# ConvNeXt-V2 block on one core: three expansions between two bursts of the convolution, statistics early, Gram in halves, a new pace for the second stage

## The chip, the cores and the metric

One core of one Trainium2 chip. The metric is device time in microseconds (us), the median over the executions of a kernel. The executions of the kernel before agree within about 0.6% in each set of measurements. Engines are named as in the profile: PE is TensorE, PEld its weight loads, ACT ScalarE, DVE VectorE, POOL GpSimd, SP SyncE.

## The reference, cut to what matters

```python
# x: 512 x 512 pixels, C = 96 channels, bf16; E = 4 * C = 384
out = depthwise_conv_3x3(x, dw)
h = layernorm_over_channels(out)          # no scale, no shift
h = gelu_tanh(h @ w1)                     # 96 -> 384
gx = sqrt(sum_over_all_pixels(h * h) + 1e-6)      # one number per channel of h
nx = gx / (mean(gx) + 1e-6)
h = grn_gamma * (h * nx) + grn_beta + h
return x + h @ w2                         # 384 -> 96
```

`gx` needs every pixel, so the kernel has two stages. Stage 1 computes `h` for the whole image for its squares, and keeps a quarter of it (half of the last two blocks). Stage 2 computes the rest of `h` anew ("recompute"), and then multiplies by `w2`.

## The kernel before

Stage 1 is a loop over slots. A slot handles four image rows (a "block") in each part of the pipeline:

- the convolution of one block on TensorE, in three bursts of 24 small matmuls into the one PSUM buffer `Y`; ScalarE then copies it to `y_bf`;
- the statistics of the layer norm (`stage_stats`), 24 small matmuls that add into the sums `S`;
- for an earlier block the expansion by `w1`: six groups of 1024 columns, called p0, p1, p2 (`pair`, GELU to `gsh`) and r0, r1, r2 (`rest`, GELU to `gm`). They go through the pool `U`, which has two buffers, so a group's matmuls wait for the GELU of the group two before;
- the squares: `bn_stats` on VectorE for most of `h`, and the diagonal of a Gram product on TensorE (`gram_mms`) for the rest. A block has 12 or 24 Gram matmuls; every third slot has 24.

`S` and `gram` are slices of one tile, `SG`.

```python
SG = psS.tile([128, 2 * NS + NCH * 128], f32, name="SG")
S = SG[:, :2 * NS].rearrange("p (h s) -> p h s", h=2)
gram = SG[:, 2 * NS:].rearrange("p (j e) -> p j e", j=NCH)
...
def burst(n):                            # convolution, 24 matmuls
    ...
    if n < 2:
        pe.drain()                       # bursts n and n+1 add to the same sums
...
def stage_moments(k):                    # once in a batch of four blocks
    dve.tensor_scalar(out=m[:, :, :N], in0=S[:, :, :N], scalar1=1.0 / C, ...)
    dve.memset(S[:], 0.0)                # the sums start anew
...
def combine(b):                          # every twelfth slot: aggregate bn_stats
    for k in sorted(bsts):
        if b == NBLK - 1 or ents[b + 1] >= 32 * (k + 1):
            for j in range(NCH):
                dve.bn_aggr(...)
```

The slot itself, in program order; each engine keeps this order in stage 1:

```python
for k in get("moments"):
    stage_moments(k)                     # at the start of the slot after the batch's last statistics
...
conv(0); pair(0); pair(1); squares(0)
conv(1); turn_x(s + 2)                   # transposes of the input on VectorE
pair(2); squares(1)
conv(2); evac()                          # y_bf
rest(0); squares(2); stage_stats(b2)
rest(1); gram_mms(b2)
rest(2); squares_rest()
combine(b)
```

Stage 2, for each block `n`: start the loads of block n + 5, add the bias to the residual on GpSimd (`xb`), then 4 groups of 12 output matmuls (`O`), each evacuated by VectorE (`o_sb`) with `xb` added. After each group, `pace` issues as many recompute units (three matmuls and one GELU of 1536 columns) as are due; a block has three.

```python
def pace(n, sub):
    due = sum(1 for v in todo if v <= n + 1) if sub == NSUB - 1 else 0
    even = LEAD + (n * NSUB + sub + 1) * (total + 2 - LEAD) / (NSUB * NBLK)
    advance(max(due, even), n + PRE)
...
for n, q in enumerate(ORDER):
    if n + PRE < NBLK:
        stage_load(n + PRE, nc.sync, nc.gpsimd)     # on GpSimd: gl (one block in three), then xr
    if n + 2 < NBLK:
        stage_xb(ORDER[n + 2], nc.gpsimd, B2c)
    o_sb = stage_mm2(n, q)                          # calls pace
```

In stage 1 all engines go through a wrapper that keeps the program's order (`InOrder`, here `pe`, `dve`, `act`, `pool`). The calls above use `nc.gpsimd` itself, so there the framework may order GpSimd's instructions as it sees fit.

Of the kernel before, what the change touches and what calls it, by code (L numbers as in the profile page):

```python
# [53 lines left out]
def kernel(  # L54
# [17 lines left out]
    E = w1.shape[1]  # L72
# [5 lines left out]
    NBLK = H // GR  # L78
# [81 lines left out]
    with ExitStack() as p1:  # L160
# [74 lines left out]
        NSUB = PXP // GPS  # L235
# [80 lines left out]
        LEAD = RES * UPB + 2  # L316
        todo = [n for n in range(NBLK) for _ in range(UPB)]
        total = len(todo)
# [10 lines left out]

        def pace(n, sub):  # L330
            due = sum(1 for v in todo if v <= n + 1) if sub == NSUB - 1 else 0
            even = LEAD + (n * NSUB + sub + 1) * (total + 2 - LEAD) / (NSUB * NBLK)
            advance(max(due, even), n + PRE)

        SG = psS.tile([128, 2 * NS + NCH * 128], f32, name="SG")
# [1 line left out]
        gram = SG[:, 2 * NS:].rearrange("p (j e) -> p j e", j=NCH)  # L337
# [15 lines left out]
        n = 0  # L353
# [54 lines left out]
        def conv_taps(b, spare):  # L408
            if spare:
                Ua = psU.tile([128, 2, W], f32, name="U")  # L410
                Ub = psU.tile([128, 2, W], f32, name="U")
                Y = [Ua[:, 0, :], Ua[:, 1, :], Ub[:, 0, :]]
            else:
                Y3 = psY.tile([128, NI, W], f32, name="Y")
                Y = [Y3[:, i, :] for i in range(NI)]
            mms = []
            for n in range(3):
                mms.append([(h, j, (n + h) % NI, dx) for dx in (0, -1, 1) for j in range(GR) for h in range(2)])
            flat = [m for ms in mms for m in ms]
            first = {}  # L420
            last = {}
            for n, (h, j, i, dx) in enumerate(flat):
                first.setdefault((i, j), n)
                last[i, j] = n

            def burst(n):
                k = sum(len(ms) for ms in mms[:n])
                for h, j, i, dx in mms[n]:
                    src = b + shift(h, j)
                    o0, o1 = max(0, -dx), W - max(0, dx)  # L430
                    pe.matmul(
                        Y[i][32 * j:32 * j + 32, o0:o1],
                        lhsT=Wq[64 * h:64 * h + 64, i, dx + 1, j, :],
                        rhs=x_rows(src, 64 * h, 64 * h + 64, i, MB * (1 + dx) + o0, o1 - o0)
                        if 0 <= src < NBLK else zrow[64 * h:64 * h + 64, o0:o1],
                        start=first[i, j] == k,
                        stop=last[i, j] == k,
                    )
                    k += 1
                if n < 2:  # L440
                    pe.drain()

            def evac():
                y = ypool.tile([128, NI, W], bf16, name="y_bf")
                if spare:
                    act.activation(out=y[:, 0:2, :], in_=Ua[:], func=ACTF.Identity)
                    act.activation(out=y[:, 2, :], in_=Ub[:, 0, :], func=ACTF.Identity)
                else:
                    act.activation(out=y[:], in_=Y3[:], func=ACTF.Identity)
                ybf[b] = y  # L450

            return [lambda n=n: burst(n) for n in range(3)], evac

        def stage_sq(b, on_act):
            q = ysqpool.tile([128, NI, W], bf16, name="ysq")
# [152 lines left out]
        def px0(b):  # L608
            return NCH * QW * (cm_quads(b) - 2)
# [51 lines left out]

            return pair, rest, squares, squares_rest, store

        def gram_mms(b):
            for k in range((TAIL - px0(b)) // E):
                for j in range(NCH):
                    c = px0(b) + k * E + j * 128
                    v = gms[b][:, c:c + 128]
                    pe.matmul(gram[:, j, :], lhsT=v, rhs=v, start=False, stop=True, skip_group_check=True)
# [51 lines left out]
        for s in range(last_slot + 1):  # L721
            get = lambda kind: at.get((s, kind), [])
            if s + 4 < NBLK:
                load_x(s + 4)
            for b in get("read"):
                stage_read(b)
            for b in get("write"):
                stage_write(b)
            for k in get("bcast"):
                stage_bcast(k)  # L730
            for k in get("rows"):
                stage_rows(k)
            if store:
                store()
                store = None
            for k in get("moments"):
                stage_moments(k)
            for k in get("newton"):
                stage_newton(k, pool)
            for b in get("norm"):  # L740
                stage_norm(b)
            for b in get("sqp"):
                stage_sq(b, False)
            for k in get("rstd"):
                stage_rstd(k, pool)
            mlp = get("mlp")

            def spread_out():
                for k in get("spread"):
                    stage_spread(k)  # L750
                for b in get("norma"):
                    stage_norm(b)

            spare = not mlp and s % 2 == 1
            taps, evac = conv_taps(s, spare) if s < NBLK else ([], None)
            if not mlp:
                for f in taps:
                    f()
                if not spare:
                    spread_out()  # L760
                if evac:
                    evac()
                for b in get("sqa"):
                    stage_sq(b, True)
                if s + 2 < NBLK:
                    turn_x(s + 2)
                for b in get("stats"):
                    stage_stats(b)
                if spare:
                    spread_out()  # L770
                for k in get("chain"):
                    stage_moments(k)
                    stage_chain(k)
                for k in get("turn"):
                    stage_turn(k)
                for b in get("gram"):
                    gram_mms(b)
            else:
                b = mlp[0]
                pair, rest, squares, squares_rest, put_out = mlp_units(b)  # L780
                conv = lambda n: taps[n]() if taps else None
                conv(0)
                pair(0)
                pair(1)
                if not taps:
                    for b2 in get("gram"):
                        if b2 != b:
                            gram_mms(b2)
                squares(0)
                conv(1)  # L790
                spread_out()
                if s + 2 < NBLK:
                    turn_x(s + 2)
                pair(2)
                squares(1)
                for k in get("turn"):
                    stage_turn(k)
                conv(2)
                if evac:
                    evac()  # L800
                rest(0)
                squares(2)
                for b2 in get("stats"):
                    stage_stats(b2)
                rest(1)
                if taps:
                    for b2 in get("gram"):
                        if b2 != b:
                            gram_mms(b2)
                rest(2)  # L810
                squares_rest()
                for b2 in get("gram"):
                    if b2 == b:
                        gram_mms(b2)
                if not is_res(b):
                    store = put_out
            if s == 1:
                setup_mlp()
            if s == 4:
                setup_rest()  # L820
            for b in get("combine"):
                combine(b)
            if s == last_slot - 3:
                pc.close()
                late.psO = p2.enter_context(tc.tile_pool(name="psO", side="right", bufs=2, space=bass.MemoryType.PSUM))
                late.xr = p2.enter_context(tc.tile_pool(name="xr", side="right", bufs=5))
                late.xb = p2.enter_context(tc.tile_pool(name="xb", side="right", bufs=3))
                late.gr = p2.enter_context(tc.tile_pool(name="gr", side="right", bufs=4))
                late.gl = p2.enter_context(tc.tile_pool(name="gld", side="right", bufs=6))
                late.o = p2.enter_context(tc.tile_pool(name="o", side="right", bufs=4))  # L830
            for n in {2: (0, 1, 2), 1: (3, 4)}.get(last_slot - s, ()):
                stage_load(n, sp, pool)
            if s == last_slot - 1:
                for n in range(RES):
                    stage_xb(ORDER[n], pool, B2bc_f)
# [104 lines left out]
```

## Time and profile before

| | before |
|---|---|
| time, median of the first measurement | 1564.21 us |
| stage 1, to the first `o_sb` | 1031.6 us |
| stage 2, from there to the end | 531.6 us |
| slots of stage 1, in turn | 7.45, 7.46, 7.63 us |
| period of `xb` on GpSimd in stage 2 | 4.09 us |

The stages and periods are read from start times in the trace. The page of the kernel before begins so (busy us, share of the span, instructions):

```profile
span 1563.2 us, 55720 instructions
...
PE 1450.2 (93%) x23749; PEld 844.8 (54%) x23749; DVE 1129.5 (72%) x2027; ACT 1447.1 (93%) x1306; POOL 1314.2 (84%) x933
```

TensorE and ScalarE are both at 93%, which does not tell what bounds a slot. ScalarE's timeline does (start, duration, engine, source line, operation, count, and in brackets the idle time before it and what ended that):

```profile
502.31 2.93 ACT L32 ACTIVATE gsh<-U 128x1024 bf16<-128x1024 f32 x3 [0.55 <-PE U L32]
505.13 1.45 ACT L32 ACTIVATE y_bf<-Y 128x1536 bf16<-128x1536 f32 x1
506.47 2.85 ACT L32 ACTIVATE gm<-U 128x1024 bf16<-128x1024 f32 x3
509.75 2.92 ACT L32 ACTIVATE gsh<-U 128x1024 bf16<-128x1024 f32 x3 [0.42 <-ACT gm L32]
```

Every slot has one hole of 0.42 to 0.56 us, before p0. The loop behind it: r2 waits for a buffer until r0's GELU is done, then TensorE does r2, burst 0 with its drain, and p0, while ScalarE has only r1 and r2 to do.

The next lines are TensorE, VectorE and ScalarE in a slot that follows aggregations.

```profile
532.31 2.92 ACT L32 ACTIVATE gsh<-U 128x1024 bf16<-128x1024 f32 x3 [0.44 <-ACT gm L32]
...
532.58 2.76 DVE L32 BATCH_NORM_AGGREGATE mv<-bst 128x2 f32<-128x192 f32 x3
...
535.26 0.23 DVE L32 TENSOR_SCALAR mom<-SG 128x128 f32<-128x128 f32 x1
...
535.59 0.17 DVE L32 MEMSET SG<- 128x128 f32 x1
...
535.81 0.44 PE L32 MATMUL SG<-rowsel,y_bf 128*128 128x4 bf16 x12 [0.28 <-DVE SG L32]
```

VectorE does the three aggregations first (2.76 us), then reads and clears the sums (`mom`, MEMSET). The clear ends 3.45 us after p0's GELU began. The statistics, which add to these sums, come just then and wait 0.28 us. Over 600 us that wait is all but nothing (us in total, times, longest):

```profile
PE SG L32 <- DVE SG L32: 2.0, 7, 0.3
```

At the end of stage 2 ScalarE starves. The pace before hands out 378 units over 512 groups, a little under three per block, so the lead of recompute over the output matmuls melts away:

```profile
1537.35 4.13 ACT L32 ACTIVATE gr<-U 128x1536 bf16<-128x1536 f32 x3 [1.40 <-PE U L32]
```

### The profile page before, as it was taken

How to read it: one execution, taken by the hardware profiler on the slowest of the kernel's cores; microseconds unless marked ns; L12 is line 12 of the kernel's file. 1: busy time of each engine (PE TensorE's matmuls, PEld its weight loads, DVE VectorE, ACT ScalarE, POOL GpSimd, SP SyncE). 2: the span in 40 equal slices, each digit the busy share in tenths (PEclk: the TensorE clock that was granted, in tenths of full speed). 3: DMA queues.
4: the chain of work that ended last, by engine and by line, in shares of the span. 5: the costliest groups of instructions: out<-in, count | busy, mean ns of one | idle time of the engine just before them, and what ended most of it. 6: DMA issues, size and time to landing. Idle time of an engine off the chain costs nothing. (4 is left out here: it accounts for less than half of the span.)

```text
span 1563.2 us, 55720 instructions
## 1 busy us (share of the span) xinstructions
PE 1450.2 (93%) x23749; PEld 844.8 (54%) x23749; DVE 1129.5 (72%) x2027; ACT 1447.1 (93%) x1306; POOL 1314.2 (84%) x933
## 2 busy tenths in 40 slices
PE   7888999999999999999999997789999999999997
PEld 3444444444444444444444444457777777777765
DVE  6748978888898888889888888855555555555544
ACT  3889989999999999999999999989999999999997
POOL 3559888998989898998889897459999999999994
PEclk9999999999999999999999999999999999999999
DMA  5668787787778677777778667869999999999993
GB/s 148 182 182 269 224 262 217 240 254 227 225 234 259 210 249 244 230 235 237 247 210 243 213 197 230 268 238 387 393 379 396 387 397 388 383 381 388 379 372 147
DMA packets 235470, 427.94 MB, mean 274 GB/s; under 512 B 34102, under 2 KB 148374, under 8 KB 235222
## 3 DMA queue, kind: packets, MB, share of 16 engines
q1 hardware_dynamic: 219972, 356.59, 70.2%
q0 software_dynamic: 13888, 67.64, 11.4%
q8 instruction: 186, 3.05, 0.8%
q14 instruction: 62, 0.51, 0.1%
q10 hardware_dynamic: 1362, 0.15, 0.1%
HBM read 272.78 MB, written 150.72 MB: 271 GB/s over the span
## 5 line engine op out<-in xcount | busy, mean ns | idle before, releaser
L32 PE MATMUL U<-ynT,w1p 128*128 128x512 bf16 x2166 | 603.1, 380 | 43.5 <-ACT gm L32 8.7
L32 DVE BATCH_NORM_STATS2 bst<-gsh 128x6 f32<-128x512 bf16 x756 | 468.7, 673 | 128.9 <-ACT gsh L32 128.4
L32 ACT ACTIVATE gr<-U 128x1536 bf16<-128x1536 f32 (+1 forms) x384 | 521.0, 1450 | 17.3 <-PE U L32 14.6
L32 POOL TENSOR_TENSOR yn<-y_bf,rbc 128x1536 bf16<-128x1536 bf16 x128 | 396.9, 3103 | 81.0 <-ACT rbc L32 29.7
L32 DVE TENSOR_TENSOR o_sb<-O,xb 128x384 bf16<-128x384 f32 x512 | 277.5, 557 | 252.2 <-PE O L32 179.7
L278 POOL TENSOR_TENSOR xb<-xr,B2c 128x1536 f32<-128x1536 bf16 x126 | 394.9, 3134 | 43.4 <-DVE B2c L32 35.2
L32 ACT ACTIVATE gsh<-U 128x1024 bf16<-128x1024 f32 x378 | 369.4, 1024 | 55.8 <-ACT gm L32 29.6
L32 ACT ACTIVATE gm<-U 128x1024 bf16<-128x1024 f32 x384 | 368.1, 1035 | 0.6 <-PE U L32 0.5
L32 PE MATMUL Y<-xT,Wq 64*32 64x511 bf16 (+1 forms) x8694 | 320.9, 388 | 9.8 <-DVE B2bc_f L32 3.7
L32 POOL TENSOR_TENSOR ysq<-y_bf 128x1536 bf16<-128x1536 bf16 x114 | 313.2, 2748 | 14.0 <-ACT y_bf L32 13.4
L32 PEld LDWEIGHTS <-w1p 128*128 128x128 bf16 x2166 | 169.4, 97 | 277.9 <-issue 174.2
L32 PEld LDWEIGHTS <-gr 128*128 128x128 bf16 x4584 | 228.7, 98 | 84.4 <-ACT gr L32 12.1
L32 PE MATMUL O<-W2s,gr 128*128 128x96 bf16 x4584 | 251.3, 206 | 12.1 <-ACT gr L32 9.4
L32 PEld LDWEIGHTS <-Wq 64*32 64x32 bf16 x9216 | 102.2, 90 | 187.5 <-issue 146.9
L32 PE MATMUL U<-w1p,ynT 128*128 128x384 bf16 (+2 forms) x1032 | 161.3, 272 | 33.7 <-ACT gm L32 30.6
L32 ACT ACTIVATE y_bf<-Y 128x1536 bf16<-128x1536 f32 x121 | 175.1, 1447 | 16.6 <-PE Y L32 16.4
L32 DVE STREAM_TRANSPOSE xT<-xin 128x576 f32<-128x576 f32 (+1 forms) x256 | 181.2, 747 | 3.2 <-DMA xin<-in_x_dram 3.1
L32 DVE BATCH_NORM_STATS2 bst<-gm 128x6 f32<-128x512 bf16 x252 | 156.5, 676 | 0.9 <-ACT gm L32 0.9
L32 PEld LDWEIGHTS <-ynT 128*128 128x128 bf16 x1032 | 88.7, 96 | 90.8 <-issue 69.4
L32 PE MATMUL SG<-gm 128*128 128x128 bf16 x2064 | 136.3, 219 | 0.5 <-ACT gm L32 0.3
L32 PEld LDWEIGHTS <-gm 128*128 128x128 bf16 x2064 | 121.0, 98 | 11.5 <-issue 0.5
L250 POOL DMA_DIRECT2D xr<-in_x_dram x123 | 67.6, 549 | 27.6 <-POOL xb L278 27.6
(103 smaller groups left out, 700.3 us busy)
## 6 DMA issues: line engine op xcount, KB each, us to landing
ynT<-yn_dram SPq DMA_DIRECT2D x254, 384.0 KB
xin<-in_x_dram SPq DMA_DIRECT2D x126, 432.0 KB
yn_dram<-yn SPq DMA_DIRECT2D x512, 96.0 KB
xr<-in_x_dram POOLq DMA_DIRECT2D x128, 384.0 KB, 6.6
out_dram<-o_sb SPq DMA_DIRECT2D x127, 384.0 KB
g_dram<-gsh SPq DMA_DIRECT2D x126, 384.0 KB
gl<-g_dram SPq DMA_DIRECT2D x84, 384.0 KB
gl<-g_dram POOLq DMA_DIRECT2D x42, 384.0 KB, 6.4
```

What stands on the lines that cost most here:

```text
L32: r = f(*a, **k)
L250: pq.dma_start(out=xr[:], in_=x[0, r0:r0 + GR].rearrange("r w c -> (r w) c").rearrange("(p g) c -> p g c", g=PXP))
L278: pq.tensor_tensor(out=xb[:], in0=grp[q]["xr"][:], in1=bias[:, None, :].to_broadcast([128, PXP, C]), op=ALU.add)
```

## The change

The intent: let three expansions stand between bursts 0 and 1. The third of them waits, by its buffer, for the GELU of the first, and that one came behind burst 0; so burst 1 is ordered behind burst 0 through ScalarE, and its drain is left out (a burst with drain takes 0.99 us in the trace before, one without 0.81; that nothing else needs the drain was the assumption). To unload TensorE in the second half of the slot, the statistics move up behind p0 and half of the Gram behind p1. In stage 2 the pace becomes three units per block exactly.

```diff
-            even = LEAD + (n * NSUB + sub + 1) * (total + 2 - LEAD) / (NSUB * NBLK)
+            even = LEAD + (n * NSUB + sub + 1) * total / (NSUB * NBLK)
...
-                if n < 2:
+                if n < 2 and fence:
                     pe.drain()
...
-                conv(0)
-                pair(0)
-                pair(1)
-                (without taps: whole gram)
-                squares(0)
+                conv(0, False)
+                pair(0)
+                stage_stats(b2)
+                pair(1)
+                squares(0)
+                gram_of_last(0)
+                pair(2)
+                squares(1)
                 conv(1)
                 spread_out()
                 turn_x(s + 2)
-                pair(2)
-                squares(1)
+                rest(0)
+                squares(2)
                 stage_turn(k)
                 conv(2)
                 evac()
-                rest(0)
-                squares(2)
-                stage_stats(b2)
                 rest(1)
-                gram_mms(b2)
+                gram_of_last(1)
                 rest(2)
                 squares_rest()
```

(Loops and conditions are left out of the diff; `gram_of_last(0)` and `(1)` are the halves.)

More of the change, by code (lines that the diff above doesn't have):

```diff
@@ L424, in conv_taps, with burst @@
                 last[i, j] = n
-            def burst(n):
+            def burst(n, fence=True):
                 k = sum(len(ms) for ms in mms[:n])
@@ L450, in evac @@
                 ybf[b] = y
-            return [lambda n=n: burst(n) for n in range(3)], evac
+            return [lambda fence=True, n=n: burst(n, fence) for n in range(3)], evac
         def stage_sq(b, on_act):
@@ L662, in mlp_units, with gram_mms @@
             return pair, rest, squares, squares_rest, store
-        def gram_mms(b):
-            for k in range((TAIL - px0(b)) // E):
+        def gram_mms(b, part=None):
+            n = (TAIL - px0(b)) // E
+            for k in range(n) if part is None else range(n // 2) if part == 0 else range(n // 2, n):
                 for j in range(NCH):
@@ L780, with gram_of_last @@
                 pair, rest, squares, squares_rest, put_out = mlp_units(b)
-                conv = lambda n: taps[n]() if taps else None
-                conv(0)
-                pair(0)
-                pair(1)
-                if not taps:
+                conv = lambda n, fence=True: taps[n](fence) if taps else None
+                def gram_of_last(part):
                     for b2 in get("gram"):
                         if b2 != b:
-                            gram_mms(b2)
-                squares(0)
+                            gram_mms(b2, part)
+                conv(0, False)
+                pair(0)
+                for b2 in get("stats"):
+                    stage_stats(b2)
+                pair(1)
+                squares(0)
+                if not taps:
+                    gram_of_last(0)
+                    gram_of_last(1)
+                if taps:
+                    gram_of_last(0)
+                pair(2)
+                squares(1)
                 conv(1)
@@ L800 @@
                     evac()
-                rest(0)
-                squares(2)
-                for b2 in get("stats"):
-                    stage_stats(b2)
                 rest(1)
                 if taps:
-                    for b2 in get("gram"):
-                        if b2 != b:
-                            gram_mms(b2)
+                    gram_of_last(1)
                 rest(2)
```

## The prediction

> **What bounds it now.** The page shows two stages. Up to about 1030 us the kernel runs steps ("slots"): one conv block, expansions p0-p2, rests r0-r2, statistics, Gram. ScalarE's timeline shows them at 7.45, 7.46, 7.63 us in turn (mean 7.51); its work back to back is 6.9 us (GELUs about 0.92 start to start, y_bf 1.34); it idles 0.42-0.56 us before p0. TensorE's timeline gives the loop behind that: r2 waits for r0's GELU (the U pool has two buffers), then r2 0.52 us, conv burst 0 with drain 1.00, 0.69 from p0's first matmul to its GELU. After 1030 us GpSimd is saturated: xb starts every 4.09 us, gaps 0.02. From about 1490 us recompute has lost its lead (it falls 0.05 units per block): output matmuls wait 1.1 us for a GELU made just before, and ScalarE idles up to 1.4 us; about 10 us are lost.
>
> **Phase 1.** One drain per slot goes (0.99 against 0.81 us for a burst). My hand schedule with these durations gives 7.54 for the old order (measured 7.51). New order:
> - p0 is prompt: r2 no longer sits just before it.
> - r0 now stands behind p2 and conv burst 1 with drain: p2 waits for p0's GELU (1.07 us into the slot), then 0.43 + 0.09 + 0.99 + 0.69: r0 is ready at 3.2, ScalarE free at 2.8. About 0.4 us of idle return there, more where Gram has 24 matmuls. Normal slots become 7.34, 7.34, 7.67: 0.09 saved on average, 9 us over some 107 slots.
> - The statistics (0.60 us) stand before p1. In the first slot of a batch of four they wait until VectorE has read and cleared the sums (mom, memset). Counted from p0's GELU, that memset ends at +0.64, +3.46 (behind three aggregations of 0.9 us) and -1.0 us in turn. The old statistics came at +3.05, so TensorE hardly waited (0.3 us, every twelfth slot); the new ones are due at -0.3. [...]p1 is stuck behind them and ScalarE starves: about 1.4 us nine times and 3.75 us eight times, 42 us.
> Phase 1: about +33 us.
>
> **Phase 2.** Recompute's pace becomes exactly 0.75 units per group of output matmuls: its lead stays near 5 units and the starving goes. ScalarE needs 1.35 x 3 = 4.05 us per block, GpSimd 4.09. The tail without recompute is longer. Net -9 us.
>
> **Sum.** 1564 + 33 - 9 = 1588 us, range 1568 to 1605.
>
> **What would show it right.** Who-waited-for-whom: SG statistics waiting for VectorE's SG rise from 2 us (300 to 900) to about 25. Slots of about 8.7 and 11 us, one each per twelve; others 7.3-7.7. ScalarE's idle moves from before p0 to before r0's gm. In phase 2 its GELUs stay back to back until about 10 groups before the end; W2s to the end is 6-12 us shorter.
>
> **What would make it wrong.** If VectorE runs less behind (its transposes move behind two pairs of bn_stats), the memset comes sooner and the loss shrinks. If r0 is less late than I reckon, normal slots reach 7.0 and the whole is level or faster. The later y_bf may slow GpSimd (about 6.7 us per slot). If the 3.7 us stall lowers TensorE's clock, it is slower still.

42 us of waits less 9 saved are the +33 of phase 1, and 1564 + 33 - 9 = 1588. That p1 does stay behind is what the profile after shows: the statistics wait until 373.89 us, and the expansion that follows them in the program starts at 374.53.

## More of the kernel before

In stage 2 GpSimd is hardly ever idle (its only holes are 0.30 us before an `xr` that follows an `xb`): a transfer (DMA_DIRECT2D) costs it about 0.55 us, an `xb` 3.13 us.

```profile
1237.08 3.14 POOL L278 TENSOR_TENSOR xb<-xr,B2c 128x1536 f32<-128x1536 bf16 x1
1240.16 0.56 POOL L245 DMA_DIRECT2D gl<-g_dram  x1
1240.71 0.54 POOL L250 DMA_DIRECT2D xr<-in_x_dram  x1
1241.26 3.14 POOL L278 TENSOR_TENSOR xb<-xr,B2c 128x1536 f32<-128x1536 bf16 x1
1244.70 0.55 POOL L250 DMA_DIRECT2D xr<-in_x_dram  x1 [0.30 <-POOL xb L278]
1245.28 3.12 POOL L278 TENSOR_TENSOR xb<-xr,B2c 128x1536 f32<-128x1536 bf16 x1
```

## The result, and the profile after

The changed kernel takes 1624.64 us (median of 4 runs, 1620.65 to 1625.98) against 1564.81 us of the kernel before in the same rounds. The ratio is 1.0369, 95% interval 1.0336 to 1.0401. Here and below a ratio is the mean time of one kernel's runs over the mean of the other's of the same rounds, so it is not quite the ratio of the medians quoted. The forecast was slower, but by 24 us, not by 60; 1624.64 lies outside the range of 1568 to 1605.

| | before | after |
|---|---|---|
| stage 1, to the first `o_sb` | 1031.6 | 1090.8 |
| stage 2 | 531.6 | 531.4 |
| ordinary slots | 7.45, 7.46, 7.63 | 7.38, 7.38, 7.66 |
| first slot of a batch, in turn | 7.4 to 7.6 | 8.3, 13.0, 7.4 |
| `xb` period | 4.09 | 4.21 |

The whole loss is in stage 1, and stage 2, which was to gain 9 us, gained nothing. The page after:

```profile
span 1622.3 us, 55623 instructions
...
PE 1466.0 (90%) x23749; PEld 865.1 (53%) x23749; DVE 1131.8 (70%) x2027; ACT 1442.9 (89%) x1306; POOL 1319.7 (81%) x933
```

ScalarE in an ordinary slot and in the one behind aggregations:

```profile
362.90 2.89 ACT L32 ACTIVATE gsh<-U 128x1024 bf16<-128x1024 f32 x3
366.20 1.02 ACT L32 ACTIVATE gm<-U 128x1024 bf16<-128x1024 f32 x1 [0.41 <-ACT gsh L32]
367.12 1.44 ACT L32 ACTIVATE y_bf<-Y 128x1536 bf16<-128x1536 f32 x1
...
370.26 1.05 ACT L32 ACTIVATE gsh<-U 128x1024 bf16<-128x1024 f32 x1
375.58 1.02 ACT L32 ACTIVATE gsh<-U 128x1024 bf16<-128x1024 f32 x1 [4.27 <-PE U L32]
377.07 1.02 ACT L32 ACTIVATE gsh<-U 128x1024 bf16<-128x1024 f32 x1 [0.47 <-PE U L32]
379.27 1.02 ACT L32 ACTIVATE gm<-U 128x1024 bf16<-128x1024 f32 x1 [1.17 <-PE U L32]
```

The ordinary slot (362.90 to 370.26, 7.36 us) has its hole before r0's `gm` instead of before p0, as forecast, and it is about as wide as the old one. The next slot has three holes: 4.27 us after p0, then 0.47, then 1.17.

All engines in that slot:

```profile
370.26 1.05 ACT L32 ACTIVATE gsh<-U 128x1024 bf16<-128x1024 f32 x1
370.66 2.77 DVE L32 BATCH_NORM_AGGREGATE mv<-bst 128x2 f32<-128x192 f32 x3
...
373.34 0.23 DVE L32 TENSOR_SCALAR mom<-SG 128x128 f32<-128x128 f32 x1
...
373.67 0.17 DVE L32 MEMSET SG<- 128x128 f32 x1
...
373.89 0.46 PE L32 MATMUL SG<-rowsel,y_bf 128*128 128x4 bf16 x12 [3.76 <-DVE SG L32]
...
376.97 1.48 PE L32 MATMUL Y<-xT,Wq 64*32 64x512 bf16 x24
...
379.10 0.87 PE L32 MATMUL Y<-xT,Wq 64*32 64x512 bf16 x24
```

TensorE came to the statistics right after p0 and waited 3.76 us for the clear of the sums; p1, which needs nothing from it, stood behind. Then burst 1 took 1.48 us, where 0.87 is the rule. The waits over the same 600 us as before:

```profile
PE SG L32 <- DVE SG L32: 27.5, 12, 3.8
```

2.0 us became 27.5 us in 12 waits. The slow burst runs at a lower clock. In stretches of this slot (busy time by engine, then the granted TensorE clock as PEclk, DMA share, GB/s):

```profile
366.00:370.00 4.00, 3.56 (x64) 1.80 (x64) 4.00 (x7) 3.80 (x4) 3.38 (x2) 1.00 1.02 320
...
374.00:377.00 3.00, 3.00 (x42) 1.61 (x43) 1.33 (x3) 1.02 (x1) 2.40 (x8) 0.50 0.63 195
...
380.00:383.00 3.00, 2.55 (x40) 1.49 (x40) 0.43 (x1) 3.00 (x4) 2.54 (x2) 1.00 0.89 255
```

The clock is halved during and after the wait: in the trace's clock record from 371.64 to 378.47 us. In each of the eight long slots it stays halved for 3.41 us (slots of 12.5 to 12.8 us) or 6.83 us (13.1 to 13.8). The record of this trace has clocks of 1.00 and 0.50 and none between.

GpSimd in stage 2, after:

```profile
1245.32 0.56 POOL L250 DMA_DIRECT2D xr<-in_x_dram  x1 [0.30 <-POOL xb L278]
1245.89 3.13 POOL L278 TENSOR_TENSOR xb<-xr,B2c 128x1536 f32<-128x1536 bf16 x1
1249.32 0.56 POOL L250 DMA_DIRECT2D xr<-in_x_dram  x1 [0.30 <-POOL xb L278]
1249.88 0.54 POOL L245 DMA_DIRECT2D gl<-g_dram  x1
1250.43 3.14 POOL L278 TENSOR_TENSOR xb<-xr,B2c 128x1536 f32<-128x1536 bf16 x1
```

Compare with the lines of before: there `gl` was issued right behind an `xb` with no wait, and `xr` behind it. Now `xr` stands first. It waits 0.30 us after the `xb` as every `xr` that follows one does, and `gl` is paid on top: from 1245.89 to 1250.43 are 4.54 us, where the old order took 4.18 us with both transfers (1237.08 to 1241.26). One block in this stage, near 1400 us, takes 7.08 us in place of 4.0: there a `gl` behind its `xr` waits 2.53 us, by the profile for output matmuls. All seven profiles with the new pace and GpSimd's order left free have this block, no other has. ScalarE at the end of stage 2 is as it was meant to be, with holes of 0.22 us in place of 1.40:

```profile
1586.43 12.34 ACT L32 ACTIVATE gr<-U 128x1536 bf16<-128x1536 f32 x9 [0.22 <-PE U L32]
```

### The profile page after: what moved, and what is told of

It is laid out like the page before. It is cut to its first block, busy times and chain, and to the rows that moved or that the text cites. A ratio compares the mean times of both kernels' runs of the same rounds, so it can differ in the third digit from the quotient of the medians. Undisturbed runs are those within 1.5% of the kernel's fastest.

```text
span 1622.3 us, 55623 instructions
## 1 busy us (share of the span) xinstructions
PE 1466.0 (90%) x23749; PEld 865.1 (53%) x23749; DVE 1131.8 (70%) x2027; ACT 1442.9 (89%) x1306; POOL 1319.7 (81%) x933
## 5 line engine op out<-in xcount | busy, mean ns | idle before, releaser
L32 PE MATMUL U<-ynT,w1p 128*128 128x512 bf16 x2166 | 627.1, 383 | 31.3 <-ACT gm L32 10.3
L32 ACT ACTIVATE gr<-U 128x1536 bf16<-128x1536 f32 (+1 forms) x384 | 519.6, 1455 | 12.5 <-PE U L32 10.5
L32 ACT ACTIVATE gm<-U 128x1024 bf16<-128x1024 f32 x384 | 378.5, 1031 | 58.1 <-PE U L32 25.4
L32 PE MATMUL Y<-xT,Wq 64*32 64x511 bf16 (+1 forms) x8694 | 328.0, 395 | 43.0 <-ACT y_bf L32 32.8
L32 PEld LDWEIGHTS <-gr 128*128 128x128 bf16 x4584 | 236.2, 98 | 109.1 <-issue 24.7
L32 PEld LDWEIGHTS <-w1p 128*128 128x128 bf16 x2166 | 175.1, 97 | 210.9 <-issue 141.1
L32 PE MATMUL O<-W2s,gr 128*128 128x96 bf16 x4584 | 256.6, 206 | 13.7 <-DVE o_sb L32 13.2
L32 PEld LDWEIGHTS <-Wq 64*32 64x32 bf16 x9216 | 114.1, 91 | 218.4 <-issue 179.7
L32 PE MATMUL U<-w1p,ynT 128*128 128x384 bf16 (+2 forms) x1032 | 163.1, 275 | 12.5 <-ACT gm L32 4.9
L32 PE MATMUL SG<-gm 128*128 128x128 bf16 x2064 | 157.3, 221 | 0.9 <-DVE SG L32 0.6
L32 PEld LDWEIGHTS <-gm 128*128 128x128 bf16 x2064 | 132.8, 99 | 40.9 <-issue 6.1
```

Source lines behind the costliest of these rows:

```text
L32: r = f(*a, **k)
```

## The experiments

**Theory.** (1) Stage 1 loses by the wait for the clear of the sums, because a writer of the sums' tile now comes early in the slot; behind aggregations the wait (3.76 us in the slot shown) brings a halved clock with it. (2) Stage 2's pace works, but the framework, which is free to order GpSimd there, has moved `gl` behind `xr`, and the longer GpSimd block eats the gain. **Rivals.** Stage 1: r0 behind the drained burst 1, the missing drain, the Gram halves, or GpSimd slowed by the later `y_bf`. Stage 2: the new pace loses by itself, or VectorE and GpSimd hinder each other.

Where these measurements count a difference only from 2% on, e2 and e3 are slower, e1, e4, e7 and e8 the same, and e10 unclear; smaller differences are read from the 95% intervals, given with each run, and from the profiles. Times are medians. "One look" is a single run with a profile, of unknown state; its stages are read from that profile.

| run | time | before | ratio | stage 1 | stage 2 | `xb` period |
|---|---|---|---|---|---|---|
| before | 1564.21 | | | 1031.6 | 531.6 | 4.09 |
| after | 1624.64 | 1564.81 | 1.0369 | 1090.8 | 531.4 | 4.21 |
| e1_pace_alone | 1563.39 | 1563.85 | 0.9995 | 1033.5 | 531.9 | 4.21 |
| e2_old_pace | 1621.49 | 1563.85 | 1.0366 | 1087.0 | 531.6 | 4.09 |
| e3_stats_late | 1609.44 | 1563.85 | 1.0256 | 1077.1 | 530.9 | 4.21 |
| e4_moments_early | 1573.20 | 1563.85 | 1.0056 | 1043.2 | 531.0 | 4.21 |
| e5_aggr_later | 1590.28 (one look) | 1566.61 | | 1056.9 | 531.6 | 4.21 |
| e6_filler | 1612.11 (one look) | 1566.61 | | 1079.3 | 531.0 | 4.21 |
| e7_pace_pinned | 1550.14 | 1566.61 | 0.9893 | 1032.9 | 514.5 | 4.03 |
| e8_before_pinned | 1564.26 | 1566.61 | 0.9972 | 1036.5 | 528.4 | 4.02 |
| e9_all_late | 1604.34 (one look) | 1565.34 | | 1071.6 | 530.9 | 4.21 |
| e10_mirror | 1536.26 | 1565.34 | 0.9804 | 1022.6 | 514.5 | 4.03 |

All ten gave the reference's result.

### e1_pace_alone and e2_old_pace: the two halves of the change

e1 is the kernel before with only this edit; e2 is the changed kernel with this edit taken back:

```diff
-  even = LEAD + (n * NSUB + sub + 1) * (total + 2 - LEAD) / (NSUB * NBLK)
+  even = LEAD + (n * NSUB + sub + 1) * total / (NSUB * NBLK)
```

> The old slot order with the new recompute pace alone. Theory (the pace holds its lead as meant, but the framework's reordering of GpSimd's stream moves the gl transfers behind the xr transfers, in 41 of 42 places as built, and GpSimd's block goes from 4.09 to 4.20 us): phase 1 as before (first o_sb at about 1032 us), phase 2 about 531 us, time 1564 within 4 us, xb period 4.20. Rival (the pace is worth 9 us or more, and only the new slot order upstream spoiled it): xb period 4.09, time 1550 to 1556.

> The new slot order with the old pace. Theory (the two parts are independent; the whole loss is in phase 1): first o_sb at about 1091 us, phase 2 about 531 us, ScalarE starving over the last 70 us as before the change, time 1624 within 5 us. Rival (the new pace loses by itself): 1612 or less.

Measured: e1 0.9995 (interval 0.997 to 1.0019), stage 2 531.9 us, `xb` every 4.21 us; e2 1.0366 (1.0345 to 1.0388), stage 1 1087.0 us. The two halves add up. The slot order carries the whole loss, and the new pace is worth nothing as it stands. As built, `gl` stands behind `xr` in 13 of 41 places with the old pace and in all 41 with the new one, in both slot orders (one further place, where `gl` stands between two `xr`, is the same in all). The number of places that changed is a fact of the built program; why the framework chose so was not looked into.

### e7_pace_pinned and e8_before_pinned: GpSimd's order kept

e7 is e1, and e8 the kernel before, with:

```diff
-  stage_load(n + PRE, nc.sync, nc.gpsimd)
+  stage_load(n + PRE, nc.sync, pool)
-  stage_xb(ORDER[n + 2], nc.gpsimd, B2c)
+  stage_xb(ORDER[n + 2], pool, B2c)
```

> The old slot order with the new pace, and GpSimd's transfers and additions of phase 2 kept in the program's order, so that every gl transfer stands before its xr transfer. Theory: xb period 4.09 us, ScalarE not starving at the end, phase 2 about 520 us, time 1552 within 3 us, faster than the kernel before by 0.5 to 1%. Rival (the order of the two transfers does not matter, phase 2 is held by the contention of VectorE and GpSimd or the DMA): xb period 4.2, time 1563.

> The kernel before with the same order kept on GpSimd and the old pace. Theory (both are needed: the order sets GpSimd's block, the pace ends the starving of the last 70 us): ScalarE starves at the end as before, time 1562 within 3 us. Rival (the order alone gives the gain): 1553 or less.

Measured: e7 0.9893 (0.9873 to 0.9913), stage 2 shorter by 17 us; e8 0.9972 (0.9949 to 0.9995), stage 2 shorter by 3 us only, with the same starving at the end (9.7 us of holes in the last 75 us; 9.8 in the kernel before, none in e7). GpSimd in e7:

```profile
1245.64 0.55 POOL L32 DMA_DIRECT2D xr<-in_x_dram  x1
1246.60 3.12 POOL L32 TENSOR_TENSOR xb<-xr,B2c 128x1536 f32<-128x1536 bf16 x1 [0.40 <-DVE o_sb L32]
1249.66 0.55 POOL L32 DMA_DIRECT2D gl<-g_dram  x1
```

More than was expected: in the program's order no `xr` waits those 0.30 us behind an `xb` any more. GpSimd now waits for VectorE instead (0.27 to 0.40 us before two of three `xb`) and no longer bounds the stage. ScalarE does: from 1100 to 1300 us it has no hole, and three GELUs, 1.343 us from start to start, make the 4.03 us of a block. Both parts are needed. Since e7 takes away these waits together with the swap of `gl` and `xr`, the swap alone was not tested. The pace alone gives 0 us, the order alone 3, the two together 17.

### e3_stats_late: the statistics back in their place

```diff
                 pair(0)
-                stage_stats(b2)
                 pair(1)
...
                 evac()
+                stage_stats(b2)
                 rest(1)
```

> The changed kernel with the statistics alone put back behind conv burst 2. Theory (the loss is the statistics' wait for VectorE's clear of the sums, with the clock loss that follows): no slot above 8 us except the known ones without conv, first o_sb at about 1031 us, granted clock about 1.0, time 1564 within 6 us. Rival (r0 behind the drained burst 1, the missing first drain or the Gram halves cost the time): long slots stay, time above 1590.

Measured: 1609.44 us, ratio 1.0256 (1.02 to 1.0312), and eight slots of 11.6 to 12.6 us. My theory in this form missed. TensorE's line in one of these slots:

```profile
364.23 0.49 PE L32 MATMUL SG<-gm 128*128 128x128 bf16 x6 [2.85 <-DVE SG L32]
```

The first half of the Gram waits 2.85 us for the clear, though it adds to other columns than those cleared. `S` and `gram` are slices of one tile; by what the framework orders them was not tested. So it is not the statistics alone: either early writer of that tile waits, and the change put two there. The batch starts without aggregations (a wait of 0.83 us in the changed kernel) lost it in e3, because there the Gram comes after the clear. One of e3's four runs took 1594.32 us at a mean granted clock of 0.990, the others 1609 to 1610 us at 0.977 or 0.978; only one of the latter was profiled, so what that run was spared is not shown.

### e4_moments_early: the clear moved instead

The sums are read and cleared in the slot of the batch's last statistics, ahead of `squares_rest` and the aggregations, no longer at the start of the next slot:

```diff
                 rest(2)
+                for k in at.get((s + 1, "moments"), []):
+                    stage_moments(k)
                 squares_rest()
```

> The changed kernel with VectorE's read and clear of the sums moved ahead of the rest-statistics and aggregations of the slot before; the statistics stay early. Theory: the 9 slots of about 13 us and the 9 of about 8.4 us vanish, all slots 7.38, 7.38, 7.66, first o_sb at about 1028 us, clock about 1.0, time 1560 within 5 us. Rival (early statistics cost by being before p1, or GpSimd is the limit): slots stay above 7.6 on average, time above 1580.

Measured: 1573.20 us, ratio 1.0056 (1.0032 to 1.008). The slots of 13 and 8.3 us are gone (from 200 us on the longest is 8.1), stage 1 is 48 us shorter than in the changed kernel. It is 13 us worse than expected. Its trace shows two reasons, worth about 10 us. Near 124 us, in the first full batch, the early statistics wait 4.7 us for GpSimd's squares `ysq`, which the old ones came late enough to miss all but 1.2 us of. And the two slots around each aggregation still take 0.8 us more in sum, since VectorE is late there: the next burst 0 waits 0.46 us for its transposes.

### e5_aggr_later and e6_filler: the length of the wait, and the clock

In e5 `combine(b)` is run after the next slot's `stage_moments`, so the clear no longer stands behind the aggregations. In e6 TensorE is given work that changes nothing during the long waits (the 17 matmuls take 3.83 us in its trace):

```diff
+                if get("moments") and taps and aggregated_in_the_slot_before:
+                    for _ in range(17):
+                        pe.matmul(Y[0], lhsT=zrow[:, :128], rhs=zrow[:], start=False, stop=False, ...)
                 stage_stats(b2)
```

> The changed kernel with the three aggregations of a slot moved behind the next slot's read and clear of the sums. Theory (the nine slots of about 13 us are long because the clear stands behind three aggregations of 0.9 us[...]): those slots become 8.3 to 8.7 us like the other batch starts, granted clock back to 0.99, phase 1 shorter by 35 to 42 us, time 1583 within 6 us. Rival (the long slots have another cause, such as the gram or GpSimd): above 1605.

> The changed kernel with 17 matmuls of zero weights on zero data (0.216 us each, adding zero to the conv sums) in front of the statistics, only in the slots whose clear stands behind aggregations, so that TensorE works through the wait instead of idling. Theory (about 1.8 us of each 13 us slot is TensorE at a lower granted clock after idling 3.8 us): clock about 1.0 there, conv burst 1 back from 1.6 to 1.0 us, those slots 11.2 us within 0.4, time 1608 within 5 us. Rival (the slow matmuls come from something else, such as DMA or PSUM conflicts): slots stay at 12.5 to 13.8 us, time 1624 within 5.

Measured: e5's slots behind aggregations take 8.4 to 8.9 us, stage 1 is 34 us shorter than in the changed kernel (35 to 42 were expected), and the time of 1590.28 lies 1 us above the range expected. One more slot of e5, near 182 us, takes 11.3 us: there the postponed aggregations came to stand before a clear, the wait was 1.96 us, and 3.41 us at half clock followed. e6's take 11.0 to 11.6 us, where the changed kernel has 12.5 to 13.8; the clock record shows no halved stretch from 159 us until the last 2 us of the run (from 370 to 378 us the mean granted clock is 1.00 in e6 and 0.60 in the changed kernel). e6 as a whole is 11.5 us shorter in stage 1. The same slot in e6, ScalarE's lines:

```profile
370.85 1.06 ACT L32 ACTIVATE gsh<-U 128x1024 bf16<-128x1024 f32 x1
375.72 1.94 ACT L32 ACTIVATE gsh<-U 128x1024 bf16<-128x1024 f32 x2 [3.81 <-PE U L32]
378.07 1.02 ACT L32 ACTIVATE gm<-U 128x1024 bf16<-128x1024 f32 x1 [0.42 <-PE U L32]
```

The first hole stays (3.81 us: the clear has not moved), but the hole of 0.47 is gone and that of 1.17 is back to 0.42. So of about 5.7 us that such a slot is too long, some 1.8 us on average are the clock and the rest, 3.9 us, is the wait itself.

### e9_all_late: what is left of the slot order

The changed kernel with statistics and whole Gram in their old places. ("The sums' bank" in what was expected is the tile `SG`.)

> The changed kernel with the statistics and the whole Gram back in their old places; what is left of phase 1's change is p2 before burst 1 and the missing first drain. Theory (no early writer of the sums' bank is left, so no wait for the clear; but statistics and Gram then crowd between burst 2 and r2, and my hand schedule gives 7.88 us per slot): no slot of 11 us or more, clock 0.99 or more, normal slots 7.8 to 7.9 on average, time 1597 within 10 us. Rival (p2 before burst 1 is worth its 0.1 us by itself): slots 7.45 on average, time 1555 to 1562.

Measured: slots of 7.67, 7.68 and 8.34 us, mean 7.90, no slot over 8.4 us from 200 us on, 1604.34 us. With p2 moved before burst 1, r0, burst 2, statistics, r1 and Gram crowd into the second half, and r2 comes too late. In a slot of 24 Gram matmuls:

```profile
353.89 1.02 ACT L32 ACTIVATE gm<-U 128x1024 bf16<-128x1024 f32 x1 [0.38 <-PE U L32]
355.28 2.85 ACT L32 ACTIVATE gsh<-U 128x1024 bf16<-128x1024 f32 x3 [0.36 <-PE U L32]
```

So with the expansions in this order the early statistics and Gram halves are needed (e4 has ordinary slots of 7.38 us with them), and they are what ran into the clear.

### e10_mirror: an order that beats both

The same device, placed one burst later: burst 0 keeps its drain, and p1, p2 and r0 stand between bursts 1 and 2; r0 waits for the GELU of p1, which stands behind burst 1, so the second drain goes. Statistics and half the Gram go before r0, the sums are cleared early as in e4, the pace and GpSimd's order are those of e7. In short:

```diff
-conv(0); pair(0); pair(1); conv(1); pair(2); conv(2); rest(0); stats; rest(1); gram; rest(2)
+conv(0); pair(0); conv(1, False); pair(1); pair(2); stats; gram half
+rest(0); conv(2); gram half; rest(1); rest(2); moments early
```

> An attempt to beat both: the drain dropped between bursts 1 and 2 instead of 0 and 1 (p1, p2 and r0 stand between them, r0 waits through ScalarE for p1), statistics and half of Gram before r0, the sums read and cleared early in the slot before, the new pace, GpSimd's order kept. My hand schedule gives 7.38 us per normal slot against 7.54 for the old order (measured 7.51), 17 us over 107 slots, of which about 7 go to the nine slots behind aggregations. Theory: normal slots 7.35 to 7.40, time 1533 to 1542. Rival (the schedule leaves out what bounds the slot, such as GpSimd at 6.7 us or VectorE behind): slots 7.5 or more, time 1550 or more.

Measured: 1536.26 us, ratio 0.9804 (0.9776 to 0.9831), slots of 7.24, 7.26 and 7.58 us, 0.15 us less on average than the kernel before. ScalarE's holes are down to 0.26 us, with another of 0.24 in the slots of 24 Gram matmuls:

```profile
356.33 1.02 ACT L32 ACTIVATE gsh<-U 128x1024 bf16<-128x1024 f32 x1
357.62 1.94 ACT L32 ACTIVATE gsh<-U 128x1024 bf16<-128x1024 f32 x2 [0.26 <-PE U L32]
...
367.05 1.02 ACT L32 ACTIVATE gm<-U 128x1024 bf16<-128x1024 f32 x1 [0.24 <-ACT gsh L32]
```

Stage 1 gained 9 us of the 17 expected: the shorter slots make about 15, but the slot near 125 us takes 12.4 us here (3.6 of them a wait for `ysq`), against 7.5 to 10.7 in the profiles of the old order. Drain, waits and Gram were not varied singly in this version, so how the gain divides among them stays open.

## Why the prediction was wrong, point by point

- **Direction and cause in stage 1: right.** The wait of the statistics for the clear, forecast from a wait of 0.3 us in the old trace, is the main loss. It was forecast to rise to "about 25" us between 300 and 900; the profile shows 27.5. e4 shows it the other way round: with the clear moved, 48 us of the 59 lost in stage 1 come back.
- **The sum.** Forecast: 33 us lost in stage 1 and 9 gained in stage 2. Measured: 59 lost and 0 gained. The slots of stage 1 make up the 59 so: 45 behind aggregations (30 forecast), 10 at the other batch starts (13), 8 at the start (none), less some 4 in ordinary slots (9).
- **The term that was mis-sized: "3.75 us eight times".** The wait itself was right (3.76). But eight slots of 12.5 to 13.8 us, mean 13.0, cost 5.7 us each over an ordinary one, 45 us in place of 30. The step that failed is the last sentence, "If the 3.7 us stall lowers TensorE's clock, it is slower still": it was named as a doubt and left out of the sum. e6 puts about 1.8 us per slot on it, which is nearly the whole difference: with the clock kept up, such a slot costs 3.9 us over an ordinary one, 3.75 was forecast.
- **"about 1.4 us nine times":** too much. These slots take 8.3 to 8.8 us, mostly 0.9 us over an ordinary one, ten times: 10 us in place of 13. VectorE was as late as forecast (the clear ends at +0.64 in eight of them) and the wait is 0.83 us there; what my schedule had too large is what it added to the wait.
- **"0.09 saved on average, 9 us":** under half. Slots of 7.38, 7.38, 7.66 were forecast to within 0.04 us, but they stand against a measured 7.51, not against my schedule's 7.54 for the old order; that is 0.04 us or some 4 us.
- **Not forecast: the start.** By the end of the first slot of the first full batch (129.0 us before, 137.1 after) 8 us are lost in this pair of profiles. 4.8 of them are that slot, where the statistics wait 3.7 us for GpSimd's `ysq` (1.2 before). The other 3 us arise in the slots before, and are not clear of the spread: that time is 129.0 to 134.1 us in the four profiles of the old slot order, and 133.5 to 138.6 in the five with early statistics.
- **Stage 2, "Net -9 us": failed.** The step was "GpSimd 4.09", taken over unchanged. It became 4.21, since the built order of `gl` and `xr` changed with the pace. The gain that was expected did arise (holes of ScalarE in the last 75 us fell from 9.8 to 1.2 us), and what took it back I estimate at 13 us: 28 more places where `gl` costs 0.36 us, and 3 us of the one block of 7.08 us. I had the changed program's order on GpSimd at hand and did not look at it in stage 2. Once the order is kept, e7 gains 17 us, more than the forecast 9, because it also removes the waits of `xr`.
- **The rivals.** r0 behind the drained burst is real (a hole of 0.41 us before its `gm`) and it is why ordinary slots gain so little, but it was in the sum. The missing drain did no harm that a run shows: all results were right, and e4, without that drain, has the ordinary slots that were forecast. The Gram half is a second early writer of the sums' tile (e3): with the statistics put back, it waits in their place. GpSimd slowed by the later `y_bf` did not keep e4's slots from 7.38 us.

## What to carry to other kernels

Before moving an instruction up on an engine that keeps the program's order (here p1 stood behind statistics that waited 3.76 us), look at when what it depends on is ready in the old trace, in every phase of the loop's cycle, and not only at its wait, which may be near zero only because it came late. Count the clock with a long wait of TensorE: half clock came with waits of 3.75 us eight times of eight here, with waits of 2.85 us eight times of eight in e3, with a wait of 1.96 us once in e5, and with none of eight gaps of 1.11 to 1.13 us in e5. And after a change of pacing compare the built instruction order on every engine that a scheduler is free to arrange: here two transfers that changed places on GpSimd go with the loss of the whole gain of a correct change.

## What the traces show of the clock, the transfers and the clear

- In the changed kernel each of the eight gaps of 3.75 to 3.76 us on TensorE came with 3.41 or 6.83 us at half clock. In e3 every one of eight gaps of 2.84 to 2.85 us (by the profile's modelled matmul ends) was followed by 3.41 or 6.83 us at half clock; in e5 eight gaps of 1.11 to 1.13 us brought none. In these traces the length of the gap does not decide by itself: the gap of 2.9 us near the long block of stage 2 was followed by half clock in three of seven profiles (e3, e5, e9, not in the changed kernel, e1, e4, e6), and one of 1.24 us at the end of stage 1 in four of twelve (in the kernel before, not in the changed one). What decides was not shown: no run was made to test it.
- In stage 2 each transfer issued by GpSimd held that engine for 0.54 to 0.56 us, and where its order was left free an `xr` behind one of its additions waited another 0.30 us (in e7 none did). That is 0.85 us of a block of 4.1 us, and the order of two transfers was worth 0.36 us.
- A matmul was made to wait for a clear of other columns of its tile; e3 shows 2.85 us of it.
